# Turning attention probabilities by 32x32 blocks and SBUF-to-SBUF transfers instead of matmuls

## The chip, the cores and the metric

The kernel runs on one core of a Trainium2 chip. The core has TensorE (PE in the profile, its weight loads PEld), VectorE (DVE), ScalarE (ACT), GpSimd (POOL) and the sequencer SP, which here issues all transfers. The metric is the device time of one execution in microseconds; the median of three runs is given.

## What is computed

Attention with rotary positions, and behind it a channel mix on the joined heads. Batch is 8, there are 8 heads, 576 positions and 64 elements a head, so the channel mix has 512 features in and 1024 inside. All is fp32.

```python
q_rot, k_rot = rotate(q), rotate(k)
scores = 1 / sqrt(D) * q_rot @ k_rot.T
scores = scores - max(scores, axis=-1)
attn = exp(scores)
attn = attn / (sum(attn, axis=-1) + 1e-09)
x = (attn @ v).transpose(0, 2, 1, 3).reshape(B, S, H * D)

x_prev = x moved by one position, zeros first
xk = mu_k * x + (1 - mu_k) * x_prev
xr = mu_r * x + (1 - mu_r) * x_prev
k = maximum(xk @ w_k, 0)
out = 1 / (1 + exp(-(xr @ w_r))) * (k * k @ w_v)
```

## The kernel before

**Order of the work.** Nothing runs in the order in which it is written. `Plan` collects operations, each with its engine or engines, a rank, a cost, what it comes after and which buffer slots it uses (`Slot`, with as many buffers for each family as `BUFS` says). `Plan.issue` then plays the program through with these costs and emits the instructions in the order in which they would start; the ready operation with the lowest rank goes first. On the chip each engine keeps this order: an instruction that has to wait holds up all behind it on its engine. `R`, `PB`, `MB` and the `B_` constants are the ranks' offsets and the biases by which an operation that two engines can do leans to one. A transfer is an operation on SP, with a planned cost of 475 ns for each issue, followed by one on the transfer engines.

**Attention.** It goes by pairs of heads, 32 pairs (8 batches of 4). `plan_prep` loads keys, queries and values of a pair and rotates them (`plan_rope`: two products with a table and a sum, on DVE or POOL). `plan_unit` works on a chunk of queries: chunks 0 to 3 have 128 queries of each head, chunk 4 the last 64 of both, one below the other. PE makes the scores (`s`, 576 keys), DVE their negative maximum (`nm`, line 391), ACT the exponentials with their sums (line 398), so there are nine tiles [128 queries, 576 keys] a pair. `plan_ratio` inverts the sums (lines 412 and 422) and scales the probabilities (line 417 on ACT, 419 on DVE).

**From probabilities to outputs.** The values product needs keys on the partitions, and the probabilities have queries there. `plan_half` does this for chunks 0 and 1 (256 queries of each head), then for 2, 3 and 4 (320). The keys of both heads together are nine blocks of 128. For each block PE turns the probabilities (line 444, two 128x128 transposes; in half 1 also the product of line 447 for chunk 4), ACT or DVE copies the result out of PSUM (`ph`, lines 248 and 250), and then one operation multiplies all nine blocks (line 464): the values, [128 keys, 64], are stationary and the turned probabilities move. The result `xT` has features on the partitions and positions along the row, as the channel mix needs it.

**Channel mix.** `plan_channel_mix` starts for a batch when its four pairs are done, in two halves of the positions (`WIDTH`, 256 and 320). `plan_mix` makes the mixed inputs, split into a high and a low part (fp32r); `plan_product` adds up three products for each block (lines 547 to 549); `plan_key`, `plan_gate` and `plan_value` do the rest, and `plan_value` stores the outputs (line 604). PE does this work of one batch between the attention work of the next.

Of the kernel before, what the change touches and what calls it, by code (L numbers as in the profile page):

```python
# [24 lines left out]
GROUPS = (5,)  # L25
PLAIN = 9
R = dict(k=36.5, q=58.68, v=133.81, csk=-374.1, csq=-277.65, csmu=-243.07, ld=29.8, rope0=-148.88, rope1=56.91,
         rope2=-70.77, split0=-47.68, split1=75.63, u0=0.8, u1=-2.05, u2=13.04, u3=7.18, u4=8.86, mx=-19.42, ex=71.39,
         rs=5.58, dg=-58.34, bd=58.2, tr=7.78, ev=20.99, av=8.35, tot=176.32, bor=34.89, m0=69.04, mh=0.49, mk=-12.58,
         mr=-5.19, ms=0.11, mx1=-16.72, mx2=10.12, mx3=33.6, mg=-0.31, mv=0.11, dr=-53.78, key0=112.28, key1=-28.76,  # L30
         key2=72.41, gate0=-44.05, gate1=69.01, wk0=-20.57, wk1=-46.23, wr0=-38.28, wr1=37.83, wv0=7.98, wv1=77.26)
PB = (-48.58, -39.33, -38.49, -5.09, -5.5, -6.69, -1.16, 1.77)
B_COPY, B_ROPE, B_SPLIT, B_LOW, B_MIX, B_SQUARE, B_RELU, B_SMALL = -24.78, 3.08, -50.61, 61.04, 1.09, 46.29, 130.32, -76.09
MB = (25.21, 20.72, 13.75, 14.61, 9.37, 5.77, 6.4, 32.33)
CY = 12
BUFS = dict(nat=2, kh=2, kl=2, qh=2, ql=2, vs=2, p=4, s=2, nm=6, sums=4, rs=4, pm=1, t=2, ph=10, xT0=4, xT1=4, last=5, raw=1, we=1, wm=1, mxf=2, mxh=6, mxl=6, acc=2, hr=2, kkh=8, kkl=8, rt=4)
# [156 lines left out]
def rope_attention_channel_mix(ctx, tc, qt, kt, v, cs_q, cs_k, mu, w_k, w_v, w_r, out):  # L193
# [17 lines left out]
    turn_k = const.tile([P, 2, S], F32, name="turn_k")  # L211
    turn_q = const.tile([P, 2, SQ], F32, name="turn_q")
# [50 lines left out]
    values_t = [const.tile([P, 10 * D], F32, name=f"values_{i}") for i in range(2)]  # L263
    for x in values_t:
        G.memset(x[:, 8 * D:10 * D], 0.0)
# [47 lines left out]
    N0 = 2 * P  # L313
    WIDTH = (N0, S - N0)
    live = {bg: {} for bg in PAIRS}

    def plan_rope(t, d, n, src, table, have, plain, load_rank):
# [27 lines left out]
    def plan_prep(t, b, g):  # L345
        d = live[b, g]
        d["plain"] = PAIRS.index((b, g)) < PLAIN
        first = PAIRS[0] == (b, g)
        plan_rope(t + R["k"], d, "k", kt[b, g], turn_k, tables["k"], d["plain"], -339.0 if first else t + R["k"] + R["ld"])
        plan_rope(t + R["q"], d, "q", qt[b, g], turn_q, tables["q"], d["plain"], -289.0 if first else t + R["q"] + R["ld"])  # L350
        d["sv"] = Slot("vs")

        x = d["vf"] = values_t[PAIRS.index((b, g)) % 2]

        def load_v():
            nc.sync.dma_start(x[:, 0:8 * D].rearrange("p (j e) -> p j e", e=D), v[b, g][:, 0:8])
            nc.sync.dma_start(x[up, 8 * D:9 * D], v[b, g][up, 8])
            nc.sync.dma_start(x[dn, 9 * D:10 * D], v[b, g][dn, 8])

        d["v"] = dma(t + R["v"] + R["ld"], P * 4 * 9 * D, load_v, [], [d["sv"]], pieces=3)  # L360

    def halves(ap):
        return ap.rearrange("p (a n) -> p a n", a=2)

    def plan_unit(t, d, c, group):
# [4 lines left out]
        s_p = d["sp", c] = Slot("p" if c < 4 else "pm")  # L370
# [12 lines left out]

        m = op("T", t, (8 if d["plain"] else 6) * (120 + 14) + (360 if c < 4 else 0), products, d["q"] + d["k"], slots + d["sq"] + d["sk"])
        for x in heads:
            s_m = Slot("nm")
            col = group["cols"].index((c, x))

            def maximum(x=x):
                w["nm", x] = sb.tile([P, 1], F32, tag="nm", name="nm", bufs=BUFS["nm"])  # L390
                V.tensor_reduce(out=w["nm", x], in_=w[x][:, :, 0:H], op=ALU.max, axis=AX.XY, negate=True)  # L391

            def exponentials(x=x, col=col):
                if "sums" not in group:
                    group["sums"] = sb.tile([P, 2], F32, tag="sums", name="sums", bufs=BUFS["sums"])
                if ("p", c) not in d:
                    d["p", c] = sb.tile([P, 2 * S] if c < 4 else [P, SQ], F32, tag="p" if c < 4 else "pm", name="p", bufs=BUFS["p" if c < 4 else "pm"])
                A.activation(halves(d["p", c][:, x * S:(x + 1) * S]), w[x][:, :, 0:H], AF.Exp, bias=w["nm", x], scale=1.0, accum_out=group["sums"][:, col:col + 1])  # L398

            o = op("V", t + R["mx"] + 0.1 * x, dve(S), maximum, [m], [slots[x], s_m])  # L400
            o = op("A", t + R["ex"] + 0.1 * x, act(S) + 230, exponentials, [o], [slots[x], s_m, s_p, group["slot"]])
            d["P", c, x] = [o]
            group["e"].append(o)

    def plan_ratio(t, d, c, group):

        w, n = {}, len(group["cols"])
        s_r, s_p = Slot("rs"), d["sp", c]

        def guard(e):  # L410
            w["r"] = sb.tile([P, 2], F32, tag="rs", name="rs", bufs=BUFS["rs"])[:, 0:n]
            (V if e == "V" else G).tensor_scalar_add(w["r"], group["sums"][:, 0:n], 1e-9)

        def scaled(e, x):
            p, r = d["p", c][:, x * S:(x + 1) * S], w["r"][:, x:x + 1]
            if e == "A":
                A.mul(p, p, r)  # L417
            else:
                V.tensor_scalar_mul(p, p, r)  # L419

        o = op({"V": (75, 0, True), "G": (200, 0, True)}, t + R["rs"], 0, guard, group["e"], [group["slot"], s_r])
        o = op("V", t + R["rs"], 80, lambda: V.reciprocal(w["r"], w["r"]), [o], [s_r])  # L422
        os = [op(one(S, B_SMALL), t + R["dg"] + 0.1 * x, 0, lambda e, x=x: scaled(e, x), [o], [s_r, s_p]) for x in range(n)]
        if c < 4:
            d["G", c, 0], d["G", c, 1], d["G", c, 4] = os[0:1], os[1:2], os
        else:
# [274 lines left out]
```

## Time and profile before

| | |
|---|---|
| median of 3 runs | 1140.24 us (1139.38 to 1140.40) |
| span of the profiled execution | 1136.0 us |
| PE busy | 1087.8 us (96%) |
| PEld busy | 931.7 us (82%) |
| DVE busy | 854.6 us (75%) |
| ACT busy | 728.5 us (64%) |
| POOL busy | 493.2 us (43%) |
| transfers on SP's queue | 70.47 MB in 35568 packets, 19.2% of 16 transfer engines |

The span runs from the first to the last instruction of the profiled execution; the profile gives no other time for it, and the runs' times lie some 4 us above the span. Rows of PE overlap, since matmuls are pipelined: their mean duration is not what each adds. Rows of the chain that ended last have the overlaps taken out. Rows of SP show how long an issue took, not the transfer.

### The profile page before, as it was taken

To read this page: it belongs to the slowest core of one execution; us is meant where nothing else is said; L and a number is where in the kernel's file an instruction comes from. 1 tells how busy PE (TensorE), PEld (TensorE's weight loads), DVE (VectorE), ACT (ScalarE), POOL (GpSimd) and SP (SyncE) were. 2 spreads that over 40 slices of the span, in tenths; PEclk is the share of its full clock that TensorE was granted. 3 is DMA by queue.
4 is the path that set the end of the run, shared out by engine and by line. 5 is a ranking of instruction groups with operands and counts; after the bars stand their busy time and mean duration, and the time that the engine had idled before them with its cause. 6 is when DMAs were issued, how large, how long until landed. Compare 5 with 4: busy or idle time off the path is not lost.

```text
span 1136.0 us, 21829 instructions
## 1 busy us (share of the span) xinstructions
PE 1087.8 (96%) x8286; PEld 931.7 (82%) x8286; DVE 854.6 (75%) x1660; ACT 728.5 (64%) x1762; POOL 493.2 (43%) x585
## 2 busy tenths in 40 slices
PE   2888999999999999999999999999999999999998
PEld 1556676788998889888988898888988898889998
DVE  6997898787677887786787777775687768876572
ACT  3676898557467767676585757666685857655242
POOL 5634666343363453454463346444263544411021
PEclk9998998999999999999999999999999999999999
DMA  5323323212111121111222101212102021100000
GB/s 210 132 89 110 132 70 101 92 55 67 44 43 55 56 73 61 51 54 37 67 65 65 55 29 60 65 55 67 56 29 90 25 78 56 49 16 7 19 20 24
DMA packets 35672, 71.86 MB, mean 63 GB/s; under 512 B 8176, under 2 KB 16368, under 8 KB 35568
## 3 DMA queue, kind: packets, MB, share of 16 engines
q1 hardware_dynamic: 35568, 70.47, 19.2%
q8 instruction: 65, 1.06, 0.4%
q14 instruction: 39, 0.32, 0.1%
HBM read 61.02 MB, written 9.44 MB: 62 GB/s over the span
## 4 chain that ended last, share of the span: by engine, by line
PE 85%; DVE 10%; ACT 3%; issue 1%; DMA 1%; POOL 0%; SPq 0%; DVEq 0%; ACTq 0%; POOLq 0%
PE acc L547 17%; PE acc L549 15%; PE acc L548 15%; PE s L382 12%; PE av L464 12%; PE t L444 11%; PE t L447 4%; DVE nm L391 2%; ACT p L398 1%; DVE wm L297 1%; DVE p L419 1%; DVE wm L296 1%; DMA turn_q<-in_cs_q 1%; ACT p L417 1%; DVE mxf L523 1%
## 5 line engine op out<-in xcount | busy, mean ns | idle before, releaser
L391 DVE TENSOR_REDUCE nm<-s 128x1 f32<-128x576 f32 x288 | 207.6, 751 | 55.4 <-PE s L382 54.5
L398 ACT ACTIVATE p<-s,nm 128x576 f32<-128x576 f32 x288 | 212.7, 742 | 52.0 <-DVE nm L391 51.5
L248 ACT COPY ph<-t 128x320 f32<-128x320 f32 (+1 forms) x378 | 147.2, 402 | 142.5 <-PE t L447 73.2
L444 PE MATMUL t<-ident,p 128*128 128x128 f32 x1152 | 221.6, 282 | 14.7 <-ACT ph L248 6.3
L464 PE MATMUL av<-ph,values 128*64 128x320 f32 (+3 forms) x1152 | 182.0, 417 | 0.7 <-ACT ph L248 0.7
L444 PEld LDWEIGHTS t<-ident,p 128*128 128x128 f32 x1152 | 148.6, 145 | 40.4 <-ACT ph L248 14.9
L547 PE MATMUL acc<-kkh,wv_h 128*128 128x320 f32 (+1 forms) x512 | 172.0, 336 | 0.8 <-DVE wv_h L250 0.8
L547 PE MATMUL acc<-mxh,wk_h 128*128 128x320 f32 (+1 forms) x512 | 172.4, 337 | 0.1
L382 PE MATMUL s<-kh,qh 64*128 64x288 f32 (+1 forms) x738 | 128.9, 400 | 26.0 <-POOL qh L244 14.6
L548 PE MATMUL acc<-mxl,wk_h 128*128 128x320 f32 (+1 forms) x512 | 151.4, 296 | 0.4 <-POOL mxl L244 0.4
L549 PE MATMUL acc<-kkh,wv_l 128*128 128x320 f32 (+1 forms) x512 | 151.6, 296 | 0.2 <-DVE wv_l L244 0.2
L549 PE MATMUL acc<-mxh,wk_l 128*128 128x320 f32 (+1 forms) x512 | 151.6, 296 | 0.0
L548 PE MATMUL acc<-kkl,wv_h 128*128 128x320 f32 (+1 forms) x512 | 151.3, 296 | 0.0
L464 PEld LDWEIGHTS av<-ph,values 128*64 128x64 f32 (+1 forms) x1152 | 86.9, 142 | 78.0 <-issue 19.7
L417 ACT ACTIVATE p<-p,rs 128x576 f32<-128x576 f32 x159 | 120.5, 774 | 46.7 <-DVE rs L422 45.7
L250 DVE COPY ph<-t 128x256 f32<-128x256 f32 (+1 forms) x198 | 87.4, 447 | 47.8 <-PE t L447 24.7
L382 PEld LDWEIGHTS s<-kh,qh 64*128 64x128 f32 (+1 forms) x738 | 74.2, 195 | 59.1 <-issue 17.9
L244 POOL TENSOR_TENSOR mxl<-mxf,mxh 128x320 fp32r<-128x320 f32 (+1 forms) x94 | 83.0, 885 | 79.9 <-ACT mxh L248 52.8
L244 POOL TENSOR_TENSOR kkl<-hr,kkh 128x256 fp32r<-128x256 f32 (+1 forms) x72 | 63.7, 886 | 112.7 <-DVE kkh L250 50.2
L547 PEld LDWEIGHTS acc<-mxh,wk_h 128*128 128x128 f32 x512 | 97.2, 190 | 7.5 <-issue 5.4
L547 PEld LDWEIGHTS acc<-kkh,wv_h 128*128 128x128 f32 x512 | 97.2, 190 | 7.2 <-issue 5.5
L523 DVE SCALAR_TENSOR_TENSOR mxf<-xT,mu_t,mxf 128x320 f32<-128x320 f32 (+1 forms) x128 | 95.8, 760 | 7.6 <-ACT mxf L518 7.1
(94 smaller groups left out, 2363.1 us busy)
## 6 DMA issues: line engine op xcount, KB each, us to landing
xq<-in_qt SPq DMA_DIRECT2D x32, 640.0 KB, 3.9
xk<-in_kt SPq DMA_DIRECT2D x32, 576.0 KB, 4.3
values<-in_v SPq DMA_DIRECT2D x32, 256.0 KB, 2.7
out_dram<-rt SPq DMA_DIRECT2D x32, 160.0 KB, 1.8
raw<-in_w_k SPq DMA_DIRECT2D x8, 512.0 KB, 4.0
raw<-in_w_v SPq DMA_DIRECT2D x8, 512.0 KB, 3.4
out_dram<-rt SPq DMA_DIRECT2D x32, 128.0 KB, 1.7
raw<-in_w_r SPq DMA_DIRECT2D x4, 512.0 KB, 3.6
```

What stands on the lines that cost most here:

```text
L244: (V if e == "V" else G).tensor_tensor(out=out, in0=a, in1=b, op=op)
L248: A.copy(out, in_)
L382: T.matmul(w[x][:, h, 0:H], lhsT=kind(d[q][r, c * P:(c + 1) * P]), rhs=kind(d[k][r, h * H:(h + 1) * H]), start=i == 0, stop=i == len(todo) ...
L391: V.tensor_reduce(out=w["nm", x], in_=w[x][:, :, 0:H], op=ALU.max, axis=AX.XY, negate=True)
L398: A.activation(halves(d["p", c][:, x * S:(x + 1) * S]), w[x][:, :, 0:H], AF.Exp, bias=w["nm", x], scale=1.0, accum_out=group["sums"][:, co ...
L417: A.mul(p, p, r)
L444: T.transpose(pt[:, x * P:(x + 1) * P], d["p", c][:, j * P:(j + 1) * P], ident)
L464: T.matmul(d["acc"][to, 0:n], lhsT=d["vf"][:, at:at + m], rhs=blocks[j][0]["h"][:, 0:n], start=j in (0, 5), stop=j == 4)
L523: V.scalar_tensor_tensor(out=x["f"], in0=d["x", half][:, 1:1 + n], scalar=mu_t[:, m:m + 1], in1=x["f"], op0=ALU.mult, op1=ALU.add)
L547: T.matmul(w["a"], lhsT=w_h[:, i, sl], rhs=x["h"], start=(i == 0), stop=False)
L548: T.matmul(w["a"], lhsT=w_h[:, i, sl], rhs=x["l"], start=False, stop=False)
L549: T.matmul(w["a"], lhsT=w_l[:, i, sl], rhs=x["h"], start=False, stop=(i == count - 1))
```

## The change

- The exponentials are written without their sums, and into another layout: `p` holds one head's four chunks, with 32 queries of each chunk side by side for every 32 keys. Chunk 4 has a tile of its own, `p4`.
- DVE turns each tile [128, 576] in place by blocks of 32x32 (`turned`).
- `plan_move` moves the blocks to where keys are on the partitions: for each head 16 SBUF-to-SBUF transfers, each of 32 partitions with 4 or 5 runs of 512 bytes, and 16 for chunk 4 with runs of 128 bytes; 48 a pair, all on SP. They end in `pt`, five blocks of 128 keys for each head (the last half filled with zeros).
- `plan_values`: the turned probabilities are stationary, [128 keys, 128 queries], and [V, 1] with 65 columns moves; the 65th column gives the sums. There are 40 such products a pair, and 10 for chunk 4. Their outputs stay in two PSUM banks of the family `t`.
- DVE adds 1e-9 to the sums, inverts them, and multiplies the outputs (4 groups of 64 columns in one operation, 5 in the other). Four PE transposes and two small products turn the outputs back, and two copies write `xT`.
- `plan_ratio`, `plan_half`, the transposes of the probabilities and their copies out of PSUM are gone.
- Keys and queries share one table, and the last 64 queries have a rotation of their own. The values of a pair come in one transfer. The halves of the channel mix are 288 and 288. The buffers are fewer in several families (`p` 3 for one head each, `pt` 2, `pt4`, `p4`, `vs`, `kl`, `ql` 1, `mxh` and `mxl` 5), and all ranks and biases have new values.

```diff
-R = dict(k=36.5, q=58.68, v=133.81, csk=-374.1, csq=-277.65, csmu=-243.07, ld=29.8, rope0=-148.88, rope1=56.91,
+R = dict(k=127.48, q=110.48, v=-783.85, cs=461.32, mu=-556.18, ld=24.35, rope0=200.29, rope1=1009.05,
...
-BUFS = dict(nat=2, kh=2, kl=2, qh=2, ql=2, vs=2, p=4, s=2, nm=6, sums=4, rs=4, pm=1, t=2, ph=10, xT0=4, xT1=4, last=5, raw=1, we=1, wm=1, mxf=2, mxh=6, mxl=6, acc=2, hr=2, kkh=8, kkl=8, rt=4)
+BUFS = dict(nat=2, kh=2, kl=1, qh=2, ql=1, vs=1, p=3, p4=1, s=2, nm=6, pt=2, pt4=1, rs=2, xq=1, t=2, xT=5, raw=1, we=1, wm=1, mxf=2, mxh=5, mxl=5, acc=2, hr=2, kkh=8, kkl=8, rt=3)
...
-    WIDTH = (N0, S - N0)
+    WIDTH = (S // 2, S // 2)
...
+        def blocks(x):
+            if c == 4:
+                if "p4" not in d:
+                    d["p4"] = sb.tile([P, S], F32, tag="p4", name="p4", bufs=BUFS["p4"])
+                return d["p4"].rearrange("p (b n) -> p b n", n=32)
+            if ("p", x) not in d:
+                d["p", x] = sb.tile([P, 4 * S], F32, tag="p", name="p", bufs=BUFS["p"])
+            return d["p", x].rearrange("p (b c n) -> p b c n", c=4, n=32)[:, :, c, :]
...
-                A.activation(halves(d["p", c][:, x * S:(x + 1) * S]), w[x][:, :, 0:H], AF.Exp, bias=w["nm", x], scale=1.0, accum_out=group["sums"][:, col:col + 1])
+            def exponentials(x=x):
+                A.activation(blocks(x).rearrange("p (a b) n -> p a b n", a=2), w[x][:, :, 0:H].rearrange("p a (b n) -> p a b n", n=32), AF.Exp, bias=w["nm", x], scale=1.0)
+
+            def turned(x=x):
+                V.transpose(blocks(x), blocks(x))
...
+    def plan_move(t, d, x):
+        sp, to = (d["sp", x] if x < 2 else d["sp4"]), Slot("pt" if x < 2 else "pt4")
+        n = P if x < 2 else 32
+        def move(a):
+            if x < 2:
+                d["pt", x] = rows_t[to.index % BUFS["pt"]]
+                dst = d["pt", x].rearrange("p (j n) -> p j n", n=4 * P)[:, :, a * P:(a + 1) * P]
+                src = d["p", x].rearrange("p (b n) -> p b n", n=P)
...
+            for s in range(4):
+                nc.sync.dma_start(dst[32 * s:32 * s + 32, 0:5 - s // 2, :], src[32 * a:32 * a + 32, s:18:4, :])
+        ready = [d["T", c, x] for c in range(4)] if x < 2 else [d["T", 4, 0]]
+        d["M", x] = [dma(t + R["dm"] + 0.1 * a, 32 * 18 * 4 * n, lambda a=a: move(a), ready, [sp, to], pieces=4) for a in range(4)]
...
+        s_av = [Slot("t"), Slot("t")]
+        def head(x):
+            pt = d["pt", x].rearrange("p (j a n) -> p j a n", a=4, n=P)
+            for a in range(4):
+                g = 2 * (a % 2) + x
+                for j in range(5):
+                    T.matmul(bank(a // 2)[:, g * G1:(g + 1) * G1], lhsT=pt[:, j, a, :], rhs=d["vf"][:, 5 * x + j, :], start=j == 0, stop=j == 4)
+        def last():
+            pt = d["pt", 2].rearrange("p (j x n) -> p j x n", x=2, n=D)
+            for j in range(5):
+                for x in range(2):
+                    T.matmul(bank(1)[(up, dn)[x], 4 * G1:5 * G1], lhsT=pt[:, j, x, :], rhs=d["vf"][:, 5 * x + j, :], start=j == 0, stop=j == 4)
...
+            def guard(i=i, parts=parts):
+                V.tensor_scalar_add(r, p[:, :, D], 1e-9)
+            def inverse(parts=parts):
+                V.reciprocal(r, r)
+            def scaled(i=i, n=n, parts=parts):
+                V.tensor_tensor(out=w["x"][:, 4 * D * i:4 * D * i + n * D].rearrange("p (g e) -> p g e", e=D), in0=p[:, :, 0:D], in1=r.unsqueeze(2).to_broadcast([P, n, D]), op=ALU.mult)
...
+        def back():
+            for a in range(4):
+                T.transpose(u["t"][:, a * P:(a + 1) * P], w["x"][:, a * P:(a + 1) * P], ident)
+        def back_last():
+            for r in (up, dn):
+                T.matmul(bank(1)[r, 384:384 + D], lhsT=w["x"][r, 512:512 + D], rhs=ident[r, r], start=True, stop=True)
+        def out(e):
+            copy(e, d["x"][:, 1:513].rearrange("p (c a n) -> p c a n", a=4, n=32), u["t"].rearrange("p (a c n) -> p c a n", a=4, n=32))
+        def out_last(e):
+            copy(e, d["x"][:, 513:S + 1], bank(1)[:, 384:384 + D])
```

More of the change, by code (lines that the diff above doesn't have):

```diff
@@ L348, in plan_prep, with plan_unit @@
         first = PAIRS[0] == (b, g)
[L349 to L353, printed above, removed]
+        plan_rope(t + R["k"], d, "k", kt[b, g], tables["cs"], d["plain"], -339.0 if first else t + R["k"] + R["ld"])
+        plan_rope(t + R["q"], d, "q", qt[b, g], tables["cs"], d["plain"], -289.0 if first else t + R["q"] + R["ld"])
+        sv = d["sv"] = Slot("vs")
         def load_v():
[L356 to L365, printed above, removed]
+            d["vf"] = values_t[sv.index % BUFS["vs"]].rearrange("p (j e) -> p j e", e=D + 1)
+            nc.sync.dma_start(d["vf"][:, :, 0:D], v[b, g])
+        d["v"] = dma(t + R["v"] + R["ld"], P * 4 * 10 * D, load_v, [], [sv])
+    def plan_unit(t, d, c):
         heads = (0, 1) if c < 4 else (0,)
@@ L400, in plan_unit @@
-            o = op("V", t + R["mx"] + 0.1 * x, dve(S), maximum, [m], [slots[x], s_m])
[L401 to L417, printed above, removed]
-            else:
[L419 to L426, printed above, removed]
-            z = op("G", t + R["bd"], 200, lambda: G.memset(d["p", 4][dn, S:SQ], 0.0), group["e"], [s_p])
-            d["G", 4, 0] = d["G", 4, 1] = os
-            d["G", 4, 4] = [op({"V": (140, 0, True), "A": (180, 0, False)}, t + R["bd"], 0, lambda e: copy(e, d["p", 4][up, S:SQ], d["p", 4][dn, 0:D]), [os[0], z], [s_p])]
@@ L499, in plan_attention @@
             plan_prep(t, *bg)
+            for x in range(2):
+                d["sp", x] = Slot("p")
+            d["sp4"] = Slot("p4")
             for c in range(5):
-                group = dict(slot=Slot("sums"), e=[], cols=[(c, 0), (c, 1)] if c < 4 else [(c, 0)])
-                plan_unit(t + R[f"u{c}"], d, c, group)
-                plan_ratio(t + R[f"u{c}"], d, c, group)
-            for half in range(2):
-                plan_half(t + 9 * half, half, d)
+                plan_unit(t + R[f"u{c}"], d, c)
+            for x in range(3):
+                plan_move(t + 0.5 * x, d, x)
+            plan_values(t, d)
     def plan_mix(t, b, half, which, f, hold):
@@ L522, in mixed @@
         def mixed(e):
-            V.scalar_tensor_tensor(out=x["f"], in0=d["x", half][:, 1:1 + n], scalar=mu_t[:, m:m + 1], in1=x["f"], op0=ALU.mult, op1=ALU.add)
+            V.scalar_tensor_tensor(out=x["f"], in0=d["x"][:, half * n + 1:half * n + n + 1], scalar=mu_t[:, m:m + 1], in1=x["f"], op0=ALU.mult, op1=ALU.add)
         def high(e):
@@ L627, in rope_attention_channel_mix @@
     tables = {
[L628 to L629 removed]
+        n: [dma(R[n], size, lambda dst=dst, src=src: nc.sync.dma_start(dst, src))]
+        for n, dst, src, size in (("cs", turns, cs, P * 8 * S), ("mu", mu_t, mu, P * 8 * NF))
     }
```

187 lines of the change are left out of this document (88 added, 99 removed).

## The prediction

> **What bounds the kernel now.** I read the page's busy shares first, then the busy time by stages, then the chain that ended last.
>
> ```profile
> span 1136.0 us, 21829 instructions
> ...
> PE 1087.8 (96%) x8286; PEld 931.7 (82%) x8286; DVE 854.6 (75%) x1660; ACT 728.5 (64%) x1762; POOL 493.2 (43%) x585
> ...
> PE 85%; DVE 10%; ACT 3%; issue 1%; DMA 1%; POOL 0%; SPq 0%; DVEq 0%; ACTq 0%; POOLq 0%
> ```
> ```profile
> 0.00:200.00 200.00, 159.17 (x961) 110.39 (x962) 170.41 (x300) 142.53 (x342) 111.49 (x124) 0.95 0.37 121
> 200.00:1060.00 860.00, 855.88 (x6784) 750.41 (x6783) 642.98 (x1275) 563.80 (x1369) 370.33 (x449) 1.00 0.17 54
> 1060.00:1136.00 76.00, 72.76 (x545) 70.93 (x543) 41.25 (x87) 22.13 (x52) 11.42 (x14) 1.00 0.06 21
> ```
> The second fence gives, for three stages, the stage and the busy time of PE, PEld, DVE, ACT and POOL. From 200 to 1060 us PE is busy 855.88 of 860 us at the full clock, with the chain on it: PE is the bound. In the first 200 us it is not: PE has 159.17, DVE 170.41 (weights are converted there). The queue that issues every transfer, SP, has 0% of the chain.
>
> The chain in order of time prices PE's pieces, each as what it adds, overlaps taken out:
>
> ```profile
> 348.82 3.04 PE av L464 x18
> ...
> 500.92 0.22 PE t L444 x2
> 501.14 0.17 PE t L447 x2
> 501.31 0.20 PE acc L547
> 501.51 0.15 PE acc L548
> ...
> 506.90 0.22 PE t L444 x2
> 507.12 0.15 PE acc L547
> ...
> 1020.70 2.51 PE av L464 x18
> ...
> 1066.66 3.04 PE av L464 x18
> ```
> Half 0 of a pair (256 queries) has nine blocks of two transposes and one values product: 9 x 0.22 + 2.51 = 4.49 us. Half 1 (320) has the L447 product besides, 0.17 and 0.05 more on the matmul behind it (0.20 against 0.15): 9 x 0.44 + 3.04 = 7.00. Together 11.5 us of PE a pair. The values products at 348.82 (pair 9) and 1066.66 (pair 31) lie 22 pairs apart: 717.84 / 22 = 32.6 us a pair. After the last one ends (1069.7) 66.3 us remain, the channel mix of the last batch.
>
> **The change on PE.** Out go the 11.5 us. In come, a pair, 40 fp32 products with 128x128 probabilities stationary and 65 columns moving, 10 with 64 columns stationary, 4 transposes back and 2 products for the last rows.
>
> ```profile
> 500.62 0.28 PEld L444 LDWEIGHTS t<-ident,p 128*128 128x128 f32 x2
> 500.87 0.30 PEld L447 LDWEIGHTS t<-ident,p 128*128 128x128 f32 x2
> 501.09 0.19 PEld L547 LDWEIGHTS acc<-mxh,wk_h 128*128 128x128 f32 x1
> ...
> L447 PEld LDWEIGHTS t<-ident,p 128*128 128x128 f32 x576 | 88.3, 194 | 0.0
> ```
> L447 is the nearest operation: fp32, 128x128 stationary, 64 columns moving. It has 576 loads for 288 products, two each, and from 500.87 to 501.09 two loads take 0.22 us: 0.11 us a load, one after the other, whatever the short passes need. So 40 x 2 x 0.11 = 8.8 us. The 20 loads of 64 columns: 1.1 us at half, 2.2 at the full price; I take 1.1, since a load's price by its columns is what is left when the passes are short. Turning back: 4 x 0.11 + 4 x 0.055 = 0.7. Sum 10.6 us (11.7 with the dear loads): PE gains 0.9 us a pair (or loses 0.2), to about 31.7 us. The 26 pairs or so behind the first 200 us give 23 us.
> The page "TensorE: Matmul & The Clock Gate" of the Trainium skill, section "Back-to-back issue gap", has about 81 ns for a load and a matmul of 128 columns in a stream; by that the 40 products would be 6.5 us. Its section "LDWEIGHTS" has columns / 1.2 ns, 107 ns here; the trace, with 0.11 us, sides with this one.
>
> **DVE, ACT, POOL.**
>
> ```profile
> L391 DVE TENSOR_REDUCE nm<-s 128x1 f32<-128x576 f32 x288 | 207.6, 751 | 55.4 <-PE s L382 54.5
> ...
> L244 DVE TENSOR_TENSOR xk<-xk 128x576 f32<-128x576 f32 x7 | 5.2, 746 | 0.0
> ...
> L250 DVE COPY ph<-t 128x256 f32<-128x256 f32 x123 | 51.2, 422 | 22.8 <-PE t L444 20.4
> ...
> L250 DVE COPY ph<-t 128x320 f32<-128x320 f32 x75 | 36.2, 489 | 25.0 <-PE t L447 24.7
> ...
> L419 DVE TENSOR_SCALAR p<-p,rs 128x576 f32<-128x576 f32 x129 | 78.8, 615 | 4.5
> ...
> L398 ACT ACTIVATION_READ_ACCUMULATOR p<-s,nm 128x1 f32 x288 | 58.2, 202 | 0.0
> ...
> L417 ACT ACTIVATE p<-p,rs 128x576 f32<-128x576 f32 x159 | 120.5, 774 | 46.7 <-DVE rs L422 45.7
> ...
> L248 ACT COPY ph<-t 128x320 f32<-128x320 f32 (+1 forms) x378 | 147.2, 402 | 142.5 <-PE t L447 73.2
> ```
> No 32x32 turn is in this trace. Both DVE operations that read 576 fp32 elements one by one take 0.75 us; a copy-like one took 0.615. I take 0.75: 288 x 0.75 = 216 us (177 to 216, more if the blocks cost extra). The division adds 64 times a guard, an inverse and a product of 256 or 320 elements out of PSUM (the 0.42 and 0.49 us of the copies, and as much again for the two small ones): about 58, an estimate. Out go 51.2 + 36.2 + 78.8 = 166, and the small operations on the sums, which the new ones replace. DVE grows by some 100 us at most, to 84% of the span, while ACT loses 58.2 + 120.5 + 147.2 = 326 and can take copies and casts. The cover is DVE's 217 us of idle time from 200 to 1060; where it is missing, in the first 200 us, six pairs at 3 us could cost 0 to 18 us. I take 0, since ACT takes over there too. POOL loses the guards and border copies and gains a 64-column piece of the query's rotation: nothing, under its 57% idle time.
>
> **The transfers.** Each pair issues 16 SBUF-to-SBUF transfers for each head and 16 for the last rows, 48, all from SP. Each has 32 partitions with 4 or 5 runs of 512 bytes (128 bytes for the last rows).
>
> ```profile
> q1 hardware_dynamic: 35568, 70.47, 19.2%
> ```
> ```profile
> q1 hardware_dynamic: 288, 0.26, 17.4%
> ```
> The first row is the whole execution. The second is the window from 211.6 to 216 us, with two stores in 1 KB packets: 0.174 x 16 x 4.4 us / 288 = 43 ns a packet. New are 32 x 48 x 144 = 221,184 packets, at most at 43 ns: 594 us an engine, 52% of the span; by bytes (84.9 MB against 70.47) 23%. With the loads' 19% the engines are no bound.
>
> Issuing is another matter:
>
> ```profile
> 1.17 0.66 SPq L325 DMA_DIRECT2D xk<-in_kt  x1
> 1.88 0.58 SPq L325 DMA_DIRECT2D xq<-in_qt  x1
> 2.51 0.43 SPq L628 DMA_DIRECT2D turn_q<-in_cs_q  x1
> 2.98 0.43 SPq L628 DMA_DIRECT2D mu_t<-in_mu  x1
> ...
> 506.50 0.47 SPq L357 DMA_DIRECT2D values<-in_v  x1
> 507.02 0.59 SPq L358 DMA_DIRECT2D values<-in_v  x1
> 507.79 0.57 SPq L325 DMA_DIRECT2D xk<-in_kt  x1
> ...
> values<-in_v SPq DMA_DIRECT2D x64, 16.0 KB, 2.3
> ```
> From start to start: 0.47 us for one run in each of 128 partitions (2.51 to 2.98), 0.52 for 64 partitions (506.50 to 507.02), 0.71 for two runs in each partition behind others (1.17 to 1.88); alone, such a one is 0.57 and the 0.04 or 0.05 to the next. The moves have several runs in each partition: I take 0.62, between ends of 0.47 and 0.71. With five other transfers a pair at 0.47 SP needs 48 x 0.62 + 2.4 = 32.2 us a pair (25.0 to 36.5). Before, it had seven at most. Against PE's 31.7 SP becomes the bound, by a hair, from 0.61 us an issue.
>
> SP also waits in order, and everything behind stands:
>
> ```profile
> SPq L604 <- DVE rt L603: 348.6, 50, 40.0
> ...
> 23.52 0.74 ACT L398 ACTIVATE p<-s,nm 128x576 f32<-128x576 f32 x1 [0.89 <-DVE nm L391]
> ```
> Of the 64 output stores 50 were waited for, 348.6 us in all, with nothing urgent behind; now moves, key and query loads stand there. And there is a loop: with three probability buffers, head 1 of the next pair writes where head 0 of this pair lies, so its exponentials wait for those 16 moves to land (2.3 us after the issue), and the next pair's first moves for its own four chunks. A queue that is full cannot make this good. I charge 1.2 us a pair, half a landing (0 to 2.3), 38 us.
>
> **The sum.** The first probabilities exist at 23.52 + 0.74 and are turned at 25 us. SP then works 32 x 32.2 = 1030 us, to 1055; the last landing, products, division and copy take 8 (2.3 and pieces as above), the last channel mix 66: 1129 us of span. The median of the three runs, 1140.2, lies 4.2 over the profiled span, which is what stands around it: 1133, and with the waits 38 more: 1171. Before, on the same footing, 1140.2.
>
> **The rivals.**
> (1) SP stays hidden and PE's gain shows: 1140 - 23 = 1117. For it: a price of 0.52 or less, as 64 partitions have (48 x 0.52 + 2.4 = 27.4 us a pair against 31.7). It decides below 0.61 us. Against: several runs in each partition, as keys have, were never under 0.57.
> (2) The loop is the bound: moves of head 0 (16 x 0.62 + 2.3 = 12.2 us) and then four chunks of the next pair in a row, at some 6 us each with PE's other work between: 36.5 us a pair. 25 + 32 x 36.5 + 8 + 66 + 4 = 1271. For it: the PE order is fixed, so a late move stops the channel mix behind it too. Against: in that order chunks of the next pair can stand ahead of this one's values products.
> (3) Loads of weights hide behind the passes, so the products cost only their columns: 3.04 us for 320 columns in ten steps (the halves of the array side by side, but for the last block) is 0.30 a step, 65 columns 0.06, 80 passes 5 us: 3.8 us a pair less, and with SP hidden 1117 - 99 = 1018. Against: the 0.11 us above.
> (4) Both effects cancel: 1138 to 1143.
>
> **How the numbers follow.** SP as the bound with some waits, 1145 to 1230: 0.50. Rival 2 and dearer issues, over 1230: 0.23. Rival 1: 0.20, rival 3: 0.02, rival 4: 0.05. A change under 0.2% (2.3 us) can't be told from none here. Faster 0.22, same 0.05, slower 0.73. The range leaves out rival 3 and the upper part of rival 2: 1110 to 1290; the likeliest case alone has 1145 to 1230.
>
> **What would show it.** Right: SP's issues stand end to end, near 0.62 us apart, from 25 us to about 70 us before the end; PE waits for transfers ahead of the values products; the weight loads there are 0.11 us apart; DVE under 85%. Wrong: issues about 0.5 us apart with gaps between pairs and PE still full (rival 1), or SP idle for long while it waits for turned probabilities (rival 2), or a turn well over 0.75 us, which would make DVE the bound.

## The result, and the profile after

The changed kernel takes 1374.7 us (median of four runs, 1367.1 to 1377.6) against 1139.8 before (1138.5 to 1140.4): a ratio of 1.205, 95% interval 1.202 to 1.209. The forecast was 1171, its range ended at 1290. The profiled execution took 1377.55 us, 1.75 more than its span.

From the page after: the span, the busy shares, the clock that PE was granted in 40 slices, the chain by engine and by line, and SP's queue.

```profile
span 1375.8 us, 24407 instructions
...
PE 1210.8 (88%) x8862; PEld 1109.6 (81%) x8862; DVE 864.4 (63%) x1496; ACT 510.1 (37%) x1015; POOL 452.1 (33%) x442
...
PEclk9998555799999999998998989998997989899999
...
q1 hardware_dynamic: 312928, 155.89, 50.9%
...
PE 48%; SPq 24%; DMA 14%; DVE 8%; issue 3%; ACT 2%; POOL 1%; ACTq 0%; DVEq 0%; POOLq 0%
SPq L439 22%; PE av L464 17%; PE s L393 9%; PE acc L579 7%; DMA xq<-in_qt 7%; PE acc L580 6%; PE acc L581 6%; DMA rows<-p 3%; DMA xk<-in_kt 3%; DVE nm L410 2%; ACT p L413 1%; DVE p L416 1%; DMA tops<-p 1%; DVE mxf L555 1%; PE av L470 1%
```

PE fell from 96% to 88% busy and from 85% to 48% of the chain; SP's issues, 0% before, are 24% of it. Line 439 is the one that issues the moves. In slices 5 to 7 (138 to 241 us) the clock is at half.

SP's order of time, in one pair of the steady part (start, how long the group took, how many issues):

```profile
628.73 0.60 SPq L373 DMA_DIRECT2D values<-in_v  x1
629.42 0.90 SPq L331 DMA_DIRECT2D xq<-in_qt  x1
630.37 20.94 SPq L439 DMA_DIRECT2D rows<-p  x28
651.41 11.05 SPq L439 DMA_DIRECT2D tops<-p  x16
662.57 0.60 SPq L331 DMA_DIRECT2D xk<-in_kt  x1
666.01 5.15 SPq L439 DMA_DIRECT2D rows<-p  x8
```

The moves stand nearly end to end: 28 in 20.94 us, with one stop inside, from 634.92 to 637.14. From start to start it is 0.645 us where nothing is waited for (the median over all moves), for the heads' runs of 512 bytes as for the last rows' of 128. From 663.17 to 666.01 SP stands still.

Where the 239.8 us of span came from is read off the values products that end a pair, with their count, the least, median and longest duration in ns, and the first and last start: pairs 9 and 31 (counted from 0, so 31 is the last) before, then after.

```profile
L464 PE MATMUL av<-ph,values x18: 432/432/537, 348.8 to 351.4; 128*64 128x320 f32 x16, 128*128 128x320 f32 x2
L464 PE MATMUL av<-ph,values x18: 432/432/537, 1066.6 to 1069.3; 128*64 128x320 f32 x16, 128*128 128x320 f32 x2
```
```profile
L470 PE MATMUL av<-values,tops x20: 219/222/271, 431.2 to 434.6; 128*64 128x65 f32 x20
L470 PE MATMUL av<-values,tops x20: 222/315/370, 1289.8 to 1293.8; 128*64 128x65 f32 x20
```

Up to pair 9: 434.6 against 351.4, 83 us. Pairs 9 to 31: 39.06 us a pair against 32.63, 22 x 6.43 = 141. The rest, the last channel mix: 82.0 against 66.7, 15. Every run below is read by these three numbers:

| run | what differs from the changed kernel | last of pair 9 at | us a pair, 9 to 31 | time |
|---|---|---|---|---|
| before | | 351.4 | 32.63 | 1139.8 |
| after | | 434.6 | 39.06 | 1374.7 |
| e2 | 12 issues a pair | 407.3 | 32.39 | 1200.9 |
| e10 | 36 issues a pair | 414.5 | 32.49 | 1210.7 |
| e17 | 42 issues a pair | 414.5 | 34.52 | 1254.8 |
| e1 | 48 issues, fewer bytes and runs | 423.5 | 36.50 | 1307.8 |
| e11 | 48 issues, long runs | 429.3 | 38.16 | 1350.3 |
| e6 | 32 issues, other buffers | 473.8 | 36.06 | 1341.6 |
| e12 | e6 with long runs | 462.9 | 35.80 | 1325.2 |
| e5 | probability buffers free at the turn | 457.9 | 38.85 | 1402.6 |
| e9 | loads issued by ACT | 445.8 | 39.21 | 1391.9 |
| e4 | half of the moves issued by ACT | 455.9 | 41.96 | 1481.8 |
| e3 | planned with 645 ns an issue | 492.5 | 38.87 | 1422.3 |
| e8 | planned with both prices | 461.7 | 38.36 | 1379.3 |
| e15 | e8 with ranks searched anew | 443.9 | 38.63 | 1367.2 |
| e7 | w_k first | 467.0 | 38.86 | 1404.0 |
| e14 | e10, w_k first | 445.7 | 32.95 | 1252.7 |
| e13 | e10, early scores made twice | 426.8 | 32.68 | 1227.1 |
| e16 | 32 issues on SP, 16 on ACT, ranks anew | 432.1 | 33.13 | 1245.2 |
| e18 | e16 with long runs | 429.4 | 32.88 | 1237.2 |

The experiments are single runs; the four runs of the changed kernel lie within 0.8%, so differences of some 10 us between two lines say nothing.

### The profile page after: what moved, and what is told of

Same layout as the page of the kernel before. It is cut to its first block, busy times and chain, and to the rows that moved or that the text cites. A ratio compares the mean times of both kernels' runs of the same rounds, so it can differ in the third digit from the quotient of the medians.

```text
span 1375.8 us, 24407 instructions
## 1 busy us (share of the span) xinstructions
PE 1210.8 (88%) x8862; PEld 1109.6 (81%) x8862; DVE 864.4 (63%) x1496; ACT 510.1 (37%) x1015; POOL 452.1 (33%) x442
## 3 DMA queue, kind: packets, MB, share of 16 engines
q1 hardware_dynamic: 312928, 155.89, 50.9%
## 4 chain that ended last, share of the span: by engine, by line
PE 48%; SPq 24%; DMA 14%; DVE 8%; issue 3%; ACT 2%; POOL 1%; ACTq 0%; DVEq 0%; POOLq 0%
SPq L439 22%; PE av L464 17%; PE s L393 9%; PE acc L579 7%; DMA xq<-in_qt 7%; PE acc L580 6%; PE acc L581 6%; DMA rows<-p 3%; DMA xk<-in_kt 3%; DVE nm L410 2%; ACT p L413 1%; DVE p L416 1%; DMA tops<-p 1%; DVE mxf L555 1%; PE av L470 1%
## 5 line engine op out<-in xcount | busy, mean ns | idle before, releaser
L464 PEld LDWEIGHTS av<-values,rows 128*128 128x128 f32 x2560 | 362.0, 229 | 27.5 <-DMA rows<-p 12.7
L464 PE MATMUL av<-values,rows 128*128 128x65 f32 x2560 | 367.0, 313 | 17.3 <-DMA rows<-p 13.6
L416 DVE STREAM_TRANSPOSE p<-p 128x576 f32<-128x576 f32 x288 | 213.8, 761 | 48.6 <-ACT p L413 40.2
L393 PE MATMUL s<-kh,qh 64*128 64x288 f32 x738 | 165.2, 484 | 71.9 <-ACT p L413 47.1
L579 PE MATMUL acc<-mxh,wk_h 128*128 128x288 f32 x512 | 166.9, 326 | 9.3 <-DVE rt L635 5.1
L579 PE MATMUL acc<-kkh,wv_h 128*128 128x288 f32 x512 | 161.6, 316 | 1.8 <-ACT rt L626 1.2
L580 PE MATMUL acc<-mxl,wk_h 128*128 128x288 f32 x512 | 158.7, 310 | 0.0
L581 PE MATMUL acc<-mxh,wk_l 128*128 128x288 f32 x512 | 158.1, 309 | 0.0
L580 PE MATMUL acc<-kkl,wv_h 128*128 128x288 f32 x512 | 153.8, 300 | 0.0
L581 PE MATMUL acc<-kkh,wv_l 128*128 128x288 f32 x512 | 153.6, 300 | 0.0
```

What stands on the lines that cost most here:

```text
L393: T.matmul(w[x][:, h, 0:H], lhsT=kind(d[q][r, c * P:(c + 1) * P]), rhs=kind(d[k][r, h * H:(h + 1) * H]), start=i == 0, stop=i == len(todo) ...
L416: V.transpose(blocks(x), blocks(x))
L464: T.matmul(bank(a // 2)[:, g * G1:(g + 1) * G1], lhsT=pt[:, j, a, :], rhs=d["vf"][:, 5 * x + j, :], start=j == 0, stop=j == 4)
L579: T.matmul(w["a"], lhsT=w_h[:, i, sl], rhs=x["h"], start=(i == 0), stop=False)
L580: T.matmul(w["a"], lhsT=w_h[:, i, sl], rhs=x["l"], start=False, stop=False)
L581: T.matmul(w["a"], lhsT=w_l[:, i, sl], rhs=x["h"], start=False, stop=(i == count - 1))
```

## Experiments: how many issues

e2 issues a quarter of the moves, e10 three quarters, e17 seven eighths. What isn't moved stays zero; PE, DVE and ACT have all their instructions.

```diff
-            for s in range(4):
+            for s in range(1):                     # e2
+            for s in range(3):                     # e10
+            for s in range(4 if a < 2 else 3):     # e17
                 nc.sync.dma_start(dst[32 * s:32 * s + 32, 0:5 - s // 2, :], src[32 * a:32 * a + 32, s:18:4, :])
```

> 12 issues a pair instead of 48: only those that fill the first 32 partitions; the rest of the turned probabilities stays zero. PE, DVE and ACT do all they do in the change. Issue theory: SP needs 12 x 0.65 + 3.4 = 11 us a pair and is no bound any more; what is left is PE with 31.7 us a pair, 1115 to 1160 us, at full clock. Rival: PE or DVE is slow by itself (half clock, 32x32 turns on DVE, PSUM banks held by the outputs); then it stays above 1230 us.

> Three quarters of the moves (row groups 0 to 2; the rest of the turned keys is left out and stays zero), buffers as in the changed kernel: 36 issues a pair. By the issue price 36 x 0.645 + 3.4 = 26.6, and with the 4.6 us of waits 31.2: just under PE's 32.4, so the pair takes 32.4 to 34 us and the time is 1200 to 1240. If something besides the number of issues holds the pair at 36 us, as it did with 32 issues and other buffers (36.1), the time is 1280 to 1320.

> Row group 3 is moved for half of the queries only: 42 issues a pair, an eighth of the moves left out. Issues take 42 x 0.645 + 3.4 = 30.5 us a pair. If the waits in SP's row (4.6 us a pair with 48) stand whatever the number of issues, the pair takes 35.1 us and the kernel 1265 to 1290. If they shrink as soon as SP has slack against PE's 32.4, the pair takes 32.5 to 33.5 us and the kernel 1205 to 1235: then the change falls over an edge between 42 and 48 issues.

From e10's page (busy shares, clock, queue, chain), and the last products of pairs 9 and 31:

```profile
PE 1127.8 (93%) x8862; PEld 1037.0 (86%) x8862; DVE 866.6 (72%) x1496; ACT 509.0 (42%) x1015; POOL 450.3 (37%) x442
...
PEclk9995555589999999999999999999999999999999
...
q1 hardware_dynamic: 257632, 136.99, 49.0%
...
PE 78%; DVE 8%; DMA 6%; SPq 3%; ACT 2%; issue 1%; POOL 1%; DVEq 0%; ACTq 0%; POOLq 0%
```
```profile
L470 PE MATMUL av<-values,tops x20: 219/222/271, 413.9 to 414.5; 128*64 128x65 f32 x20
L470 PE MATMUL av<-values,tops x20: 219/222/272, 1128.7 to 1129.3; 128*64 128x65 f32 x20
```

With 36 issues a pair the moves cost nothing in the steady part: 32.49 us against 32.39 with 12, SP has 3% of the chain, and PE runs at the full clock, with the transfer engines as busy (49.0%) as in the changed kernel. The last 12 issues cost 6.6 us a pair, 164 us in all. The price of an issue and 3.4 us for the other five (0.58 to 0.74 each from start to start) give 26.6 us of issues with 36, 30.5 with 42 and 34.4 with 48. Measured are 32.49 (PE), 34.52 and 39.06: once SP is the bound, its waits come on top, 4.0 and 4.7 us. e17 fell between its two forecasts: with some slack the waits shrink, but little. In three other orders of the same work (e3, e8 and e15 below) they are 4.0 to 4.5 us. e2 came out above its forecast of 1115 to 1160, since it reached pair 9 56 us later than before; that loss has a section of its own.

e1 keeps the 48 issues and gives each one run in a partition (the rest of the keys stays zero); e11 moves all bytes, but with keys grouped so that a run has 4 or 5 blocks (2048 or 2560 bytes).

```diff
-                nc.sync.dma_start(dst[32 * s:32 * s + 32, 0:5 - s // 2, :], src[32 * a:32 * a + 32, s:18:4, :])
+                nc.sync.dma_start(dst[32 * s:32 * s + 32, 0:1, :], src[32 * a:32 * a + 32, s:s + 1, :])      # e1
+            for s, (at, m) in enumerate(((0, 5), (5, 5), (10, 4), (14, 4))):                               # e11
+                nc.sync.dma_start(d["pt", x][32 * s:32 * s + 32, 5 * n * a:5 * n * a + m * n], src[32 * a:32 * a + 32, at * n:(at + m) * n])
```

> Still 48 issues a pair, but each moves one run per partition where the change moves 4 or 5; the other blocks of the turned probabilities stay zero. It tells the cost of an issue from the cost of the bytes. Issue theory (SP's 48 issues set the time): if an issue keeps its 0.65 us, 31 + 3.4 us a pair remain and only the waits behind loads go, so 1290 to 1350 us; if one run makes an issue cheaper (0.52 as for the 64-partition loads of before), 28.4 us a pair and PE is the bound, 1120 to 1180. Byte theory (the transfer engines' 51% delay the key and query loads and SP stands behind them): the 2.6 us a pair of SP's stalls inside the moves go, and 1290 or less with issues still at 0.65. Loop theory (head 1's exponentials wait for head 0's moves to land): no more than 20 us.

> 48 issues and all the bytes, but the keys are grouped so that each partition's run is 4 or 5 blocks in one piece (2048 or 2560 bytes, for the last rows 512 or 640): 1536 packets a pair instead of 4608 (the last rows' products are 20 of 32 columns instead of 10 of 64). If the number of packets makes SP wait for earlier transfers, the pair falls to about 36.5 us, as with one run in each partition, and the time to 1300 to 1325. If it is the bytes, it stays at 1360 to 1380.

SP's queue in e1, then in e11:

```profile
q1 hardware_dynamic: 140896, 89.83, 24.7%
```
```profile
q1 hardware_dynamic: 140896, 155.89, 44.9%
```

An issue of one run in a partition takes 0.633 us from start to start, in e1 as in e11, against 0.645 with four or five: the price hangs little on the runs and not on the bytes. Half of the transfer engines' share is worth 2.6 us a pair (e1), long runs with all bytes 0.9 (e11, which fell between its two forecasts, 1300 to 1325 and 1360 to 1380). Of both, the cheaper issue alone is 48 x 0.012 = 0.6 us. e1 moves fewer bytes (89.83 MB) than e10 (136.99) and is 4.0 us a pair slower, so the bytes are not what the 48 issues cost.

## Experiments: what SP waits for

Three of the largest waits of SP after (us in all, times, longest), then those of ACT's exponentials for moves to land:

```profile
SPq L636 <- DVE rt L635: 67.0, 11, 20.8
SPq L439 <- DVE p L416: 39.7, 13, 6.1
SPq L439 <- DMA xq<-in_qt: 25.7, 15, 2.6
```
```profile
ACT p L413 <- DMA rows<-p: 61.7, 25, 4.3
ACT p L413 <- DMA tops<-p: 59.1, 14, 6.3
```

The stores' row (line 636) belongs to the two ends: between 434.6 and 1293.8 us it is 1.4 us, the other two are 26.0 and 25.7. The second fence is the loop of the prediction's second rival: a probability buffer is taken until its moves have landed. e5 lets the moves read a constant table, after the same turns, and no longer hold the buffers, so that these are free at once. e9 gives three loads a pair to ACT.

```diff
-                src = d["p", x].rearrange("p (b n) -> p b n", n=P)
+                src = turns.rearrange("p i n -> p (i n)").rearrange("p (b n) -> p b n", n=P)               # e5, likewise for p4
-        d["M", x] = [dma(t + R["dm"] + 0.1 * a, 32 * 18 * 4 * n, lambda a=a: move(a), ready, [sp, to], pieces=4) for a in range(4)]
+        d["M", x] = [dma(t + R["dm"] + 0.1 * a, 32 * 18 * 4 * n, lambda a=a: move(a), ready, [to], pieces=4) for a in range(4)]   # e5
-            nc.sync.dma_start(m["x"][:, :, 0:w], src)
+            A.dma_start(m["x"][:, :, 0:w], src)                                                            # e9, likewise the values
```

> The moves read a constant table instead of the turned probabilities (so the outputs are made of other numbers); number, size, place in the order and the wait for the turns stay. What goes is that a probability buffer stays taken until its 16 moves have landed. If these landings are what adds the 4.6 us a pair to the 34.4 us of issues, the pair comes down to 34.5 to 36 us and the time to 1230 to 1290. If SP's waits come from its own slots for transfers in flight behind key and query loads, the pair stays at 38 to 39 us: 1345 to 1380.

> The key, query and value loads (three issues a pair) are issued by ACT; SP keeps the 48 moves and the two stores: 31.0 + 1.2 us of issues a pair. If it is SP's total of issues and of the waits that stand in its row that holds the pace, the pair falls from 39.1 to 33 to 36 us and the time to 1180 to 1280. If the pace comes from the landings of the moves and the order of the chunks, the pair stays at 38 to 40: 1350 to 1400, or more if the loads hold up exponentials on ACT.

e5: 38.85 us a pair. The loop is real, but it isn't what holds the pace; the time, 1402.6, lies above its forecasts because pair 9 came 23 us later. e9: 39.21, though SP has 2.1 us a pair fewer of issues. Its waits grew by as much:

```profile
SPq L439 <- DVE p L416: 41.9, 11, 6.6
SPq L439 <- DMA xk<-in_kt: 41.4, 22, 3.5
SPq L439 <- DMA xq<-in_qt: 26.0, 21, 3.8
SPq L439 <- DMA values<-in_v: 17.1, 13, 3.1
```

Moves wait here for the landing of loads whose data they don't use (84 us in the last three rows). What connects them is the program: all its transfers report their landing on eight semaphores in turn, and an issue waits until the transfer that last used its semaphore has landed. In the trace of after 1699 of SP's 1718 issues wait for the very semaphore that they then use; the stop inside the 28 moves above is one, where the query load issued at 629.42 landed at 637.13, and the eighth issue behind it started at 637.14. In e9 SP and ACT share the eight, so that the loads on ACT's queue still stop SP's moves.

Eight issues at 0.645 us are 5.2 us, and a query load now often takes longer than that to land. The page's issues, with KB each and the median us from issue to landing, before and then after:

```profile
xq<-in_qt SPq DMA_DIRECT2D x32, 640.0 KB, 3.9
```
```profile
xq<-in_qt SPq DMA_DIRECT2D x32, 640.0 KB, 6.1
```

So e9 did not take the loads' waits out of SP's row, and the plain sum "issues plus a fixed wait" fails there. Of the 4.7 us a pair above the issues' price after, between pairs 9 and 31, issues that last longer than the usual 0.60 us are 2.0, waits for such a semaphore 1.3, and waits for turned probabilities and other work 1.0. What lengthens those issues is open; so is what more semaphores would bring, since no run has them. In e5 and e9 the wait that was taken away was replaced by others.

e6 lets chunk 4 ride with head 0's moves (runs of 640 bytes, 32 issues); head 0 then has one buffer and head 1 two, in the same space. e12 adds the long runs.

```diff
-                d["p", x] = sb.tile([P, 4 * S], F32, tag="p", name="p", bufs=BUFS["p"])
-            return d["p", x].rearrange("p (b c n) -> p b c n", c=4, n=32)[:, :, c, :]
+                d["p", x] = sb.tile([P, (5 - x) * S], F32, tag=f"p{x}", name="p", bufs=BUFS[f"p{x}"])
+            return d["p", x].rearrange("p (b c n) -> p b c n", c=5 - x, n=32)[:, :, c, :]
```

> Chunk 4 rides with head 0's moves (runs of 640 bytes), so a pair has 32 issues instead of 48; all the work and the bytes are as before, and head 0's buffer now waits for chunk 4 too. By the issue price: 32 x 0.645 + 3.4 = 24 us of issues a pair, less than PE's 32.4, so the period falls to 33 to 36 us: 1200 to 1290, with the ramp's loss kept. If the landing loop or the packets are the bound rather than the issues, the period stays at 37 to 39: 1320 to 1375.

> Both: 32 issues a pair and long runs (up to 3200 bytes), all the work. Against 1341.6 with 32 issues and short runs: if what is left there is transfers in flight, 1280 to 1320; if it is the buffers (head 0's single probability buffer, the single values buffer that SP waited for 176 us), 1330 to 1345.

e6 misses its forecast by the issues: 36.06 us a pair where 36 issues with the old buffers have 32.49. Its SP stands for the values buffer instead:

```profile
SPq L370 <- PE av L459: 175.9, 25, 16.9
```

The merge bought its issues with buffers, as far as this goes: e16 below, with 32 issues on SP and the old buffers, has 33.13, but its order is another too. With long runs (e12) it is 35.80 us a pair, and 1325.2 lies between the two cases forecast: transfers are a small part of what is left.

## Experiments: two queues, and the plan

e4 gives half of the moves to ACT, those of odd `a`. e3 and e8 tell the planner the measured prices (645 ns an issue; e8 also 4.5 us for a head's products instead of 2.4), and in e15 all ranks and biases were searched anew with these. e16 gives ACT the last rows' moves alone, with both prices and a search of its own.

```diff
-        o = self.op("S", rank, 475 * pieces, fn, after, uses)
+        o = self.op("S", rank, 645 * pieces, fn, after, uses)                                              # e3, e8, e15, e16, e18
-        o = [op("T", t + R["av"] + 0.1 * x, 20 * 2 * 58 + 100, lambda x=x: head(x), d["M", x] + [d["v"]], s_av + [d["sv"], d["spt", x]]) for x in range(2)]
+        o = [op("T", t + R["av"] + 0.1 * x, 20 * 2 * 111 + 100, lambda x=x: head(x), d["M", x] + [d["v"]], s_av + [d["sv"], d["spt", x]]) for x in range(2)]   # e8, e15, e16, e18
-                nc.sync.dma_start(dst[32 * s:32 * s + 32, 0:5 - s // 2, :], src[32 * a:32 * a + 32, s:18:4, :])
+                (A if a % 2 else nc.sync).dma_start(dst[32 * s:32 * s + 32, 0:5 - s // 2, :], src[32 * a:32 * a + 32, s:18:4, :])   # e4
+                (A if x == 2 else nc.sync).dma_start(dst[32 * s:32 * s + 32, 0:5 - s // 2, :], src[32 * a:32 * a + 32, s:18:4, :])  # e16
```

> The plan charges 645 ns for an issue instead of 475; the work is the same, only the order of instructions changes. Issue theory: SP's own work is a floor, first move at 45 us, 31 pairs of 34.4 us, 85 us behind the last move: 1197 us plus waits; with an order that knows the price perhaps 1230 to 1330. If the order made for 475 ns costs most of the loss (plan theory), it falls below 1230. If the waits come from the loop or from loads in front of the moves, it stays within 20 us of 1375.

> Half of the moves are issued by ACT, half by SP; all data is moved. SP then has 24 x 0.65 + 3.4 = 19 us a pair, ACT its 510 us and 24 x 0.65 x 32 = 500 us more. Issue theory with a price for each queue: neither is the bound, 1120 to 1200 us. If both queues share what makes an issue slow, the sum of both is still 31 us a pair and it stays above 1300. Loop theory: the landing of a head comes after 5 us instead of 10, so it gains as well, but less than 80 us.

> The planner gets two measured prices: 645 ns instead of 475 for an issue and 4.5 us instead of 2.4 for a head's products. If part of the loss is an order planned with wrong prices, the time falls to 1300 to 1350. If SP's pace is all, or the ranks suit the old prices, it stays at 1365 to 1425, as with the issue price alone (1422).

> All the work, 48 issues; the planner has the measured prices (0.645 us an issue, 4.5 us a head's products) and its ranks and biases were searched anew for them; it plans 1238 us. If order and ranks caused most of the loss, 1240 to 1300. If SP's 34.4 us of issues a pair and half clock in the ramp hold, which a plan can't take away, 1300 to 1360.

> All the work; the 16 moves of the last rows are issued by ACT, 32 stay on SP (24 us a pair with the others), and the ranks were searched anew for the measured prices; the planner has 1183 us. If SP's issues are the bound and ACT can carry 10 us of issues a pair in this order, 1180 to 1240, the best of the full versions; if ACT's waits for the turns hold up the exponentials as with 24 issues on ACT, 1300 or more. Neither theory puts it under the time before.

> The re-planned kernel with the last rows' moves on ACT (1245.2), and its keys grouped into long runs: all the work, a third of the packets. If transfers in flight still cost it something (moves were 9 per cent of its chain), 1220 to 1240; if PE and the ramp are all that is left, 1240 to 1250. It stays above the time before.

No plan takes SP's row away: 38.4 to 38.9 us a pair in e3, e8 and e15. e15 planned 1238 us and took 1367, above both its forecasts, as e3 was with 1422. e4 is the worst of all, though its SP issues half as much: an issue takes ACT 0.6 us too, ACT stands 134 us in all in front of its moves, which holds up its exponentials, and these wait for buffers that come free later. How much of the loss each is was not tried. In ACT's waits of e4 the landings grew against the fence above:

```profile
ACT p L413 <- DMA rows<-p: 162.9, 33, 15.7
ACT p L413 <- DMA tops<-p: 144.5, 24, 20.7
```

e16 shares the work out better: only the last rows' 16 moves on ACT, and ranks made for that (which of the two did it, no run tells). It does everything the kernel must do in 33.13 us a pair, with PE as the bound again:

```profile
PEclk9995665877999999999999999999999999999999
...
PE 70%; DMA 8%; DVE 8%; ACT 4%; ACTq 3%; SPq 2%; POOL 2%; issue 2%; DVEq 0%; POOLq 0%
```

It took 1245.2 us, 1.09 times its neighbour of before (1139.9), 5 over its forecast's upper end; e18, with long runs, 1237.2. These are the best full versions, and both are slower than before: most of what they lose lies ahead of pair 9 (80.7 and 78 us) and behind pair 31 (15.8 and 15.9).

## Experiments: the first 250 us

Even e10 reaches pair 9 63 us late. In 100 to 264 us, busy time of PE, PEld, DVE, ACT and POOL, then the granted clock, the transfer engines' share and GB/s; before, then e10, then e13:

```profile
100.00:264.00 164.00, 153.08 (x1042) 117.51 (x1040) 137.63 (x251) 122.54 (x303) 89.33 (x103) 0.97 0.26 83
```
```profile
100.00:264.00 164.00, 135.08 (x638) 109.12 (x639) 107.98 (x187) 49.16 (x78) 49.30 (x46) 0.54 0.52 128
```
```profile
100.00:264.00 164.00, 132.55 (x747) 105.33 (x746) 106.29 (x187) 46.86 (x72) 45.41 (x42) 0.73 0.53 128
```

In e10 PE is 82% busy there at half clock, and it leads the chain. Pieces of it:

```profile
69.08 8.72 PE av L464 x40
...
178.47 2.95 PE s L393 x8
181.41 8.72 PE av L464 x40
190.14 2.27 PE s L393 x8
192.41 0.75 DVE nm L410
```

A head's 20 products, each in two passes (x40), take 8.72 us here, from the first pairs on, and 4.4 to 4.7 later. (The recorded clock of e10 reads full until it first falls at 90 us, which the piece at 69.08 belies.) Two causes were tried. e7 and e14 load and convert w_k first (e7 with 48 issues, e14 with 36), since the first product of the channel mix came at 254.8 us after and 99.2 before. e13 is e10 with each score product of the first seven pairs made twice into the same place.

```diff
-         ... wk0=9.83, wk1=-474.97, wr0=258.55, wr1=-384.1, wv0=-453.03, wv1=-214.08)
+         ... wk0=-475, wk1=-300, wr0=-250, wr1=-100, wv0=0, wv1=170)                                        # e7, e14
...
+        d["early"] = PAIRS.index((b, g)) < 7                                                                # e13
...
-            for i, (q, k) in enumerate(todo):
...
+            for again in range(2 if d["early"] else 1):                                                     # e13
+                for i, (q, k) in enumerate(todo):
```

> Only the ranks of the weights are changed: w_k first, then w_r, then w_v, so that the first channel mix can start near 100 us instead of 255. If the 83 us lost up to pair 9 come from the late channel mix, 30 to 60 us of them come back: 1315 to 1345. If SP's issues hold the pace from the first move to the last, nothing comes back: 1365 to 1380.

> The 36-issue kernel with the weights in another order (w_k first, then w_r, w_v), with no queue as the bound. If the ramp is lost because no channel mix fills PE until 250 us, the first mix near 95 us brings 15 to 50 us: 1160 to 1195. If a first mix that then lacks w_r and w_v until 270 us only stops the order, it is 1205 to 1240, as the same order brought nothing with 48 issues.

> The 36-issue kernel (1210.7; a quarter of the moves left out), in which every score product of the first seven pairs is made twice over: 40 more products of 288 columns a pair, 4.7 us of PE at the full clock, 9.4 at half. If the ramp's loss is PE at half clock because its work there is mostly weight loads with 65 columns moving, the added products keep the clock up and the kernel gets faster by more work: the half-clock stretch (138 to 264 us) shrinks and the time is 1165 to 1200. If the clock has nothing to do with it, or the gaps keep it low all the same, it is 1225 to 1260.

The late mix alone is not the cause: with it at 93.6 (e7) and 92.3 us (e14), pair 9 came 32 and 31 us later still. By its time e13 belongs to the second case of its forecast (1227.1, in 1225 to 1260), in which the clock has no part or stays low, yet the clock answered: 7 x 4.7 = 33 us of added work (at the full clock) cost 16. The clock between 100 and 264 us rose from 0.54 to 0.73 with PE no busier and its pauses no shorter (16 of over 0.3 us in either run, 28.8 us in e10 and 30.8 in e13), and some heads' products there ran at the full clock:

```profile
215.32 8.72 PE av L466 x40
...
233.73 4.65 PE av L466 x40
```

So between these two runs the clock followed what PE does, and not how long it is busy: it stayed at half through products that load 128 columns for 65 that move, and was higher with more scores, where 288 columns move. That isn't all of it: without pauses, from 264 us on, the same heads' products run at the full clock in e10, and before, the stretch of 100 to 264 us had only 8.6 us of such pauses. The page "TensorE: Matmul & The Clock Gate" of the Trainium skill, section "What's actually happening", has the full clock after some 3.4 us of sustained activity; the trace doesn't agree for these products, 8.72 us without a gap at half clock. An estimate of what the half clock costs e10 here is 135.08 x (1 - 0.54) = 62 us of PE's time, about what is lost; that it is the cause was not shown, since no run had the same work at the full clock.

## Why the prediction was wrong, point by point

- PE's new price was right. Pieces of the chain after, at the full clock:

```profile
603.44 4.68 PE av L464 x40
...
658.20 4.41 PE av L464 x40
...
667.39 0.73 PE av L470 x20
...
670.32 0.26 PE av L510 x4
670.58 0.59 PE t L506 x4
```

Two heads and the rest are 10.4 to 10.9 us a pair (10.6 forecast), by weight loads 0.11 us apart (4.41 us for 40); rival 3 is out. The removed 11.5 was too high. The chain of before between pairs 9 and 31, by line, has 32.9% in the three lines, 10.7 us a pair:

```profile
by line: PE acc L547 18.7%; PE av L464 16.0%; PE acc L549 15.8%; PE acc L548 15.8%; PE s L382 14.1%; PE t L444 12.3%; PE t L447 4.6%; ACT p L398 0.9%; DVE p L419 0.4%; DVE nm L391 0.3%; DVE rs L412 0.3%; ACT p L417 0.2%; issue 0.2%; ACT ph 
```

So PE's gain is not 0.9 us a pair but 0.24 (32.63 to 32.39 in e2). There was next to nothing to win.
- DVE was right: a turn takes 761 ns (0.75 forecast), DVE is 63% busy and no bound; its busy time grew by 10 us, where 100 at most was forecast.

```profile
L416 DVE STREAM_TRANSPOSE p<-p 128x576 f32<-128x576 f32 x288 | 213.8, 761 | 48.6 <-ACT p L413 40.2
```

- The transfer engines are no bound, as said, at 50.9% with the loads (bounds 42 to 71). Their price shows only in landings.
- SP as the bound was right, its row in the sum too short. An issue: 0.645 for 0.62. That it came so near was luck: 0.62 was taken for the several runs in a partition, but with one run an issue still comes every 0.633 us (e1), and the query loads of before, two runs in a partition like the keys', mostly lasted 0.33 to 0.35. The other five: 3.4 us for 2.4. Waits: 4.5 for 1.2. From the first move at 45.1 to the last at 1290.8 are 1245.7 us, 38.9 a pair, against 33.4: 32 x 5.5 = 177 us, 70 from the issues and 107 from the waits. The step that failed most is the waits: half a landing for one loop, 1.2 us, where the row had 4.5 to 4.7, from longer issues, earlier transfers that hold a semaphore, and turned probabilities. Ten of the 32 pairs lie ahead of 434.6 us, where e10 with a quarter fewer issues is only 20 us earlier; that part of the 177, some 55 us, isn't SP's alone.
- "First moves at 25 us" became 45, since head 0's moves need all four chunks turned and not the first tile; "0 to 18 us, taken as 0" for the first 200 us became 63 even without SP as the bound. The prediction looked for that loss in DVE alone and gave PE's work there no price by the clock. The end took 85 us from the last move instead of 74. Start and end are 31 us; 177 + 31 less 2.5 around the span are the 206 between 1171 and the profiled 1377.6.
- The rivals: the second's number, 36.5 us a pair, came nearest, but its mechanism fell with e5. The first decides where it was put, by issues against PE, and e10 shows it: but SP hidden gives 1210.7, not 1117, because of the ramp, the end and a gain of 0.24.

## What to carry to other kernels

Price a transfer twice: what it takes on the transfer engines, and what its issue takes on the queue in front of them. Here 36 small ones a pair, 26.6 us of issues beside 32.4 of PE, cost nothing; at 42, 30.5 us, they cost 2 us a pair, and at 48, 34.4 us, 6.6. So a queue is full before its issues alone fill the time, since everything on it waits in order. Ask too what lets an issue start: with eight semaphores in turn, one slow load stops the eighth issue behind it. And ask a stage with pauses twice, for its work and for its clock: in the first 250 us here weight loads for few moving columns went with half the clock, and what that cost is only estimated.

## What had not been expected of the hardware

- An issue on SP takes 0.59 or 0.60 us and comes 0.633 to 0.645 after the one before, for one run or five in each of 32 partitions, for 128, 512 or 2560 bytes. On ACT it takes 0.61 (e4), and comes 0.66 after the one before (e16, the median).
- Moves waited for loads of other data to land (84 us in e9), even for those of another queue. That is the program's doing, by the eight semaphores that its transfers share, and not the chip's.
- In the first 250 us a head's products, back to back for 8.72 us, ran at half clock throughout; the same engine, no busier, had 0.73 instead of 0.54 with twice the scores.
- Larger runs from SBUF to SBUF (a third of the packets) were worth 0.9 us a pair where SP is the bound, 0.6 of it the cheaper issue. Where SP isn't, e18 is 8 us under e16, which two single runs can't show.
